# Transposing the second half of x block 0 in the DMA crossbar instead of on TensorE

## The chip, the cores and the metric

The kernel runs on one core of one Trainium2 chip. The metric is device time in microseconds (us) of one execution. The kernel before takes 291.47 us (median of four runs, 291.16 to 291.76).

## The reference

```python
# x: (1, 2048, 576), w1: (576, 4608), b1: (4608), w2: (4608, 576), b2: (576), all bfloat16
def reference(x, w1, b1, w2, b2):
    h = jnp.einsum("bsd,df->bsf", x, w1) + b1
    zero = jnp.zeros_like(h)
    r = jnp.where(h > zero, h, zero)
    h = r * r
    out = jnp.einsum("bsf,fd->bsd", h, w2) + b2
    return out
```

It is two dense layers with a squared ReLU between them. The 2048 rows of x are worked through in four blocks of 512 rows.

## The kernel before

For the first layer TensorE needs x transposed, with the 576 columns of x on partitions. Blocks 1 to 3 come transposed by the DMA crossbar, long before they are needed. Block 0 is needed at once. Its four row tiles of 128 rows come by plain loads, TensorE transposes them (five transposes of 128x128 for each row tile), and VectorE and ScalarE copy the results from PSUM into the tile `xT0`.

```python
    load_x(nc.sync, 0)              # row tile 0 of x, on SyncE's queue
    load_x(nc.scalar, 1)            # row tile 1, on ScalarE's queue
    load_w1n(nc.sync, 0)            # w1n: first 512 columns of w1, one load for each 128 rows
    load_x(nc.scalar, 2)
    load_w1n(nc.sync, 1)
    load_x(nc.sync, 3)
    for k in range(2, NK):          # NK is 4
        load_w1n(nc.sync, k)
# ... cut: b1, b2 loads on GpSimd's queue, constants ...
                def part(h, k):     # half h (256 rows) of block 0, contraction rows k*128 ...
                    hc = slice(h * HS, (h + 1) * HS)
                    for g in range(G):
                        keep(nc.tensor.matmul(banks[g][:, hc], lhsT=w1n[:, k, g * P:(g + 1) * P],
                                              rhs=xT[:, O + k, hc], ...))   # 128x256
                for j in range(2):
                    for k in range(NK):
                        x_transpose(j, k)
                for j in range(2):
                    x_transpose(j, NK)
                x_copies(0)
                part(0, 0)
                for k in range(NK + 1):
                    x_transpose(2, k)
                part(0, 1)
                part(0, 2)
                for k in range(NK + 1):
                    x_transpose(3, k)
                x_copies(1)
                dup_windows(0)
                part(0, 3)
                part(1, 0)
                make_b1T()
                for k in range(1, NK):
                    part(1, k)
# ... then four matmuls over the last 64 rows of w1 (weights w1n8, 64x512), called half-row
#     matmuls below; then a_rows: the rest of layer 1 with the weights w1_h (w_h in the profile)
# ... cut: the loads of w1_h, w1n8, later x blocks and w2, all on SyncE's queue ...
```

A load is *issued* by an engine's queue, which keeps that engine's sequencer busy for some tenths of a microsecond, and it *lands* some microseconds later, when its semaphore has been counted up. SyncE and ScalarE together use eight such semaphores in turn, so the ninth load waits at its issue for the first to land.

## Time and profile before

| | before |
|---|---|
| time, median | 291.47 us |
| span in the profile | 289.8 us |
| TensorE busy | 285.1 us (98%) |
| TensorE transposes of x | 20 |
| first half-row matmul starts | 9.77 us |
| first w_h matmul starts | 10.21 us |

First, lines of the profile's page of the kernel before: the span, the busy time of each engine, the share of each engine in the chain of work that ended last, one group of matmuls (`w1n` parts, with busy time, mean ns of one, and idle time before them), and one group of DMA issues (KB each, median us from issue to landing).

```profile
span 289.8 us, 4679 instructions
...
PE 285.1 (98%) x2017; PEld 133.7 (46%) x2032; DVE 79.5 (27%) x176; ACT 95.2 (33%) x152; POOL 2.8 (1%) x11
...
PE 98%; issue 0%; DVE 0%
...
L228 PE MATMUL pn<-xTw,w1n 128*128 128x256 bf16 x32 | 4.8, 304 | 0.0
...
w1n<-in_w_dram SPq DMA_DIRECT2D x4, 128.0 KB, 3.7
```

The chain is TensorE alone, so only TensorE work removed, or TensorE idle made, moves the time. The 32 half-width matmuls had no idle time before them (0.0).

The timeline of TensorE at the start. The columns are start, us covered, engine, line, operation, output and inputs, shapes, number. A bracket at the end would name idle time and what ended it; there is none.

```profile
3.49 1.25 PE L150 MATMUL tb<-ident,x_sb 128*128 128x128 bf16 x10
4.59 1.01 PE L228 MATMUL pn<-xTw,w1n 128*128 128x256 bf16 x4
5.40 0.74 PE L150 MATMUL tb<-ident,x_sb 128*128 128x128 bf16 x5
5.93 1.39 PE L228 MATMUL pn<-xTw,w1n 128*128 128x256 bf16 x8
7.16 0.44 PE L150 MATMUL tb<-ident,x_sb 128*128 128x128 bf16 x5
7.44 1.04 PE L228 MATMUL pn<-xTw,w1n 128*128 128x256 bf16 x8
...
8.37 1.47 PE L228 MATMUL pn<-xTw,w1n 128*128 128x256 bf16 x12
9.77 0.39 PE L204 MATMUL pn<-xTw,w1n 64*128 64x512 bf16 x1
...
10.21 0.38 PE L189 MATMUL ph<-xTw,w_h 64*128 64x512 bf16 x1
```

From the first part at 4.59 to the half-row matmuls at 9.77 it is 5.18 us. The ten transposes of row tiles 2 and 3 (the two lines x5) take 0.81 us of it in the chain of waits; the 32 matmuls take the other 4.37 us.

Last, windows of one microsecond each. The columns are the busy share of TensorE, its weight loads, VectorE, ScalarE and GpSimd (with numbers of instructions), then the granted TensorE clock, the DMA share and the GB/s. The DMA share adds up the times that packets took, so with packets of two queues in flight on one engine it can pass 1. The clock column needs care at the start: it prints 1.00 wherever the trace has no clock record, and the first record of this trace starts at 6.65 us. Until then TensorE ran at half rate here, as the durations show: up to 6.57 us each 128x256 matmul starts 213 ns after the one before it, from 6.83 us on 109 ns; the transposes follow each other after 107 ns at first and after 56 ns in the last five. So 15 of the 20 transposes and 8 of the 32 matmuls ran at half rate, although the first window prints 1.00.

```profile
4.00:5.00 1.00, 1.00 (x10) 0.86 (x9) 0.51 (x3) 0.65 (x2) 0.00 (x0) 1.00 0.85 231
6.00:7.00 1.00, 1.00 (x9) 0.77 (x7) 0.00 (x0) 0.00 (x0) 0.18 (x1) 1.00 1.17 272
9.00:10.00 1.00, 1.00 (x11) 0.62 (x10) 0.84 (x2) 0.00 (x0) 0.00 (x0) 1.00 0.73 178
```

### The profile page before, as it was taken

How to read it: one execution, taken by the hardware profiler on the slowest of the kernel's cores; microseconds unless marked ns; L12 is line 12 of the kernel's file. 1: busy time of each engine (PE TensorE's matmuls, PEld its weight loads, DVE VectorE, ACT ScalarE, POOL GpSimd, SP SyncE). 2: the span in 40 equal slices, each digit the busy share in tenths (PEclk: the TensorE clock that was granted, in tenths of full speed). 3: DMA queues.
4: the chain of work that ended last, by engine and by line, in shares of the span. 5: the costliest groups of instructions: out<-in, count | busy, mean ns of one | idle time of the engine just before them, and what ended most of it. 6: DMA issues, size and time to landing. Idle time of an engine off the chain costs nothing.

```text
span 289.8 us, 4679 instructions
## 1 busy us (share of the span) xinstructions
PE 285.1 (98%) x2017; PEld 133.7 (46%) x2032; DVE 79.5 (27%) x176; ACT 95.2 (33%) x152; POOL 2.8 (1%) x11
## 2 busy tenths in 40 slices
PE   8999999999999999999999999999999999999996
PEld 5544444444444444444444444444445444444454
DVE  1644554444502100000025444444440000000001
ACT  2666666666500000000027666666670000000000
POOL 3000000000000000000000000000000000000000
PEclk9999999999999999999999999999999999999999
DMA  7999999400001000000000000000000200000000
GB/s 198 213 235 185 315 388 234 83 0 2 0 19 33 5 20 18 18 18 20 18 18 2 1 2 0 2 0 2 0 2 0 38 18 18 18 20 18 20 18 20
DMA packets 30581, 16.26 MB, mean 56 GB/s; under 512 B 14676, under 2 KB 30560, under 8 KB 30560
## 3 DMA queue, kind: packets, MB, share of 16 engines
q1 hardware_dynamic: 30176, 15.65, 21.7%
q8 instruction: 16, 0.26, 0.4%
q10 hardware_dynamic: 288, 0.30, 0.4%
q14 instruction: 5, 0.04, 0.0%
q0 software_dynamic: 96, 0.01, 0.0%
HBM read 11.36 MB, written 2.36 MB: 47 GB/s over the span
## 4 chain that ended last, share of the span: by engine, by line
PE 98%; issue 0%; DVE 0%
PE po L293 43%; PE ph L189 42%; PE pt L272 5%; PE pn L210 4%; PE pn L228 1%; PE wps L63 1%; PE tb L150 1%; PE ph L191 1%; PE pn L204 1%; DVE o_sb L295 0%; PE b1T_ps L167 0%; PE pn L206 0%
## 5 line engine op out<-in xcount | busy, mean ns | idle before, releaser
L191 PE MATMUL ph<-xTw,w_h 64*128 64x512 bf16 x576 | 124.6, 376 | 0.0
L189 PE MATMUL ph<-xTw,w_h 64*128 64x512 bf16 x576 | 124.6, 376 | 0.0
L293 PE MATMUL po<-w_sb,hT 128*128 128x512 bf16 (+2 forms) x600 | 123.8, 366 | 0.8 <-issue 0.3
L177 ACT ACTIVATE r<-ph,b1T 128x512 bf16<-128x512 f32 x128 | 81.0, 684 | 41.7 <-PE ph L191 41.7
L293 PEld LDWEIGHTS <-hT 128*128 128x128 bf16 x612 | 58.3, 98 | 66.7 <-issue 0.8
L189 PEld LDWEIGHTS <-w_h 64*128 64x128 bf16 x576 | 54.1, 94 | 68.3
L178 DVE TENSOR_TENSOR hT<-r 128x512 bf16<-128x512 bf16 x144 | 61.1, 425 | 75.9 <-ACT r L177 75.4
L191 PEld LDWEIGHTS <-w_h 64*128 64x128 bf16 x576 | 54.1, 94 | 0.0
L295 DVE TENSOR_TENSOR o_sb<-po,b_bc 128x512 bf16<-128x512 f32 (+2 forms) x17 | 11.2, 660 | 125.0 <-PE po L293 125.0
L177 ACT ACTIVATE r<-pn,b1T 128x512 bf16<-128x512 f32 x16 | 10.3, 687 | 68.7 <-PE pn L206 67.4
L272 PE MATMUL pt<-hT,w_sb 128*64 128x512 bf16 x144 | 15.9, 380 | 0.0
L272 PEld LDWEIGHTS <-w_sb 128*64 128x64 bf16 x144 | 8.0, 110 | 7.8 <-issue 0.8
L210 PE MATMUL pn<-xTw,w1n 128*128 128x512 bf16 x45 | 10.4, 379 | 0.4 <-issue 0.3
L210 PEld LDWEIGHTS <-w1n 128*128 128x128 bf16 x48 | 4.5, 98 | 6.0 <-issue 0.8
L275 ACT ACTIVATE oT<-pt,b2T 128x512 bf16<-128x512 f32 x2 | 1.4, 687 | 14.5 <-PE pt L272 14.5
L228 PE MATMUL pn<-xTw,w1n 128*128 128x256 bf16 x32 | 4.8, 304 | 0.0
L228 PEld LDWEIGHTS <-w1n 128*128 128x128 bf16 x32 | 3.4, 110 | 0.6
L63 PE MATMUL wps<-const-bfloat16-1.0 128*128 128x512 bf16 (+1 forms) x7 | 2.8, 581 | 0.8 <-PEq L346 0.8
L157 DVE COPY xTw<-tb 128x256 bf16<-128x256 bf16 x4 | 1.1, 292 | 6.6 <-PE tb L150 6.6
L120 DVE COPY xTw<-xTw 64x2048 bf16<-64x2048 bf16 x4 | 2.8, 690 | 0.2
L121 DVE COPY xTw<-xTw 64x2048 bf16<-64x2048 bf16 x4 | 2.7, 687 | 0.1
L159 ACT COPY xTw<-tb 128x256 bf16<-128x256 bf16 x4 | 1.3, 375 | 3.7 <-PE tb L150 3.7
(23 smaller groups left out, 16.9 us busy)
## 6 DMA issues: line engine op xcount, KB each, us to landing
w_sb<-in_w_dram SPq DMA_DIRECT2D x6, 864.0 KB, 9.6
w_h<-in_w_dram SPq DMA_DIRECT2D x14, 288.0 KB, 6.8
out_dram<-o_sb SPq DMA_DIRECT2D x15, 128.0 KB, 1.7
w_h<-in_w_dram SPq DMA_DIRECT2D x4, 144.0 KB, 3.6
w1n<-in_w_dram SPq DMA_DIRECT2D x4, 128.0 KB, 3.7
x_sb<-in_x_dram ACTq DMA_DIRECT2D x2, 144.0 KB, 2.8
x_sb<-in_x_dram SPq DMA_DIRECT2D x2, 144.0 KB, 3.3
out_dram<-ot SPq DMA_DIRECT2D x4, 64.0 KB, 1.8
```

What stands on the lines that cost most here:

```text
L63: keep(nc.tensor.matmul(wps[:, 0:n], lhsT=ones[:, 0:P], rhs=ones[:, 0:n], start=True, stop=True))
L150: keep(nc.tensor.transpose(bank[:, slot, qc], xs[:, j, c0:c0 + P], ident[:]))
L177: keep(nc.scalar.activation(out=r[:], in_=bank[:], func=ACT.Relu, bias=b1T[:, ft:ft + 1], scale=1.0))
L178: keep(nc.vector.tensor_tensor(out=hTs[sb][:, ft, :], in0=r[:], in1=r[:], op=ALU.mult))
L189: keep(nc.tensor.matmul(bx[:], lhsT=w1_h[0:H, LO_C[i], jc], rhs=xT[0:H, LO_W[i], :], start=(i == 0), stop=(i == NC - 1)))
L191: keep(nc.tensor.matmul(by[:], lhsT=w1_h[H:P, UP_C[i], jc], rhs=xT[H:P, UP_W[i], :], start=(i == 0), stop=(i == NC - 1)))
L204: keep(nc.tensor.matmul(banks[2 * i][:], lhsT=w1n8[0:H, i, :], rhs=xT[0:H, SPC, :], start=start, stop=stop, skip_group_check=order == "k_o ...
L210: keep(nc.tensor.matmul(banks[g][:], lhsT=w1n[:, k, g * P:(g + 1) * P], rhs=xT[:, O + k, :], start=start, stop=stop))
L228: keep(nc.tensor.matmul(banks[g][:, hc], lhsT=w1n[:, k, g * P:(g + 1) * P], rhs=xT[:, O + k, hc], start=(h == 0 and k == 0), stop=False, s ...
L272: keep(nc.tensor.matmul(pt[h * DT:(h + 1) * DT, :], lhsT=w2_sb[:, ft, DM:D], rhs=hTs[sb + h][:, ft, :], start=(i == 0), stop=(i == NFT - 1)))
L293: keep(nc.tensor.matmul(po[:, 0:d1 - d0], lhsT=hT[:, ft, jj * P:(jj + 1) * P], rhs=w2_sb[:, ft, d0:d1], start=(i == 0), stop=(i == NFT - 1)))
L295: keep(nc.vector.tensor_tensor(out=o_sb[:, d0:d1], in0=po[:, 0:d1 - d0], in1=b2_bc[:, d0:d1], op=ALU.add))
```

## The change

The intent: TensorE is the bound, and ten of its transposes (0.81 us) are work that the DMA crossbar can do. Rows 256 to 511 of block 0 now come by two transposing loads on ScalarE's queue (256 KB and 64 KB), straight into `xT0`. The two plain loads of these rows go, and so do the copies from PSUM. The GpSimd loads of b1 and b2 move to other queues.

```diff
+    HS = SB // 2
+    alloc_xT(0)
+    xT0 = xT_blk[0]
     load_x(nc.sync, 0)
     load_x(nc.scalar, 1)
-    load_w1n(nc.sync, 0)
-    load_x(nc.scalar, 2)
-    load_w1n(nc.sync, 1)
-    load_x(nc.sync, 3)
-    for k in range(2, NK):
+    keep(nc.scalar.dma_start_transpose(out=xT0[:, O:O + NK, HS:SB], in_=x2[HS:SB, 0:P * NK]))
+    keep(nc.scalar.dma_start_transpose(out=xT0[:, E3:E3 + 1, HS:SB], in_=x2[HS:SB, D - P:D]))
+    for k in range(NK):
         load_w1n(nc.sync, k)
@@ (cut)
-    nc.gpsimd.dma_start(out=b1_rows[0:NFT, :], in_=b1.rearrange("(ft p) -> ft p", p=P))
-    (the two b2 loads on nc.gpsimd: moved behind the w1 loads on nc.sync)
+    keep(nc.scalar.dma_start(out=b1_rows[0:NFT, :], in_=b1.rearrange("(ft p) -> ft p", p=P)))
@@ (cut: PSUM banks of the transposes regrouped; all copies now on VectorE)
-                (transposes of row tiles 2 and 3 between the parts, x_copies(1))
+                for k in (0, 1, 3, 2, NK):
+                    for j in range(2):
+                        x_transpose(j, k)
+                x_copies()
                 dup_windows(0)
-                part(0, 3)
+                for k in (0, 1, 3, 2):
+                    part(0, k)
                 part(1, 0)
                 make_b1T()
```

More of the change, by code (lines that the diff above doesn't have):

```diff
@@ L57 @@
     ps_o = ctx.enter_context(tc.tile_pool(name="ps_o", bufs=4, space=PSUM))
-    wps = ps_o.tile([P, 512], FP32, name="wps", tag="po")
+    wps = ps_h.tile([P, 512], FP32, name="wps", tag="ph")
     ones = nc.const_aps.tensor(1.0, [P, 512], BF16)
@@ L63 @@
         keep(nc.tensor.matmul(wps[:, 0:n], lhsT=ones[:, 0:P], rhs=ones[:, 0:n], start=True, stop=True))
-    xs = const.tile([P, RT, D], BF16, name="x_sb")
+    xs = const.tile([P, RT // 2, D], BF16, name="x_sb")
     w1n = wpool.tile([P, NK, GW], BF16, name="w1n")
@@ L83, in load_w1, with alloc_xT @@
                       in_=w1_v[:, :, GW + h * FH + j0 * P:GW + h * FH + j1 * P]))
+    HS = SB // 2
+    xT_blk = {}
+    def alloc_xT(sb):
+        xT_blk[sb] = xtpool.tile([P, NC, SB], BF16, name="xTw", tag="xTw")
+    E3, O, SPC, E = 0, 1, 5, 6
+    alloc_xT(0)
+    xT0 = xT_blk[0]
     load_x(nc.sync, 0)
     load_x(nc.scalar, 1)
-    load_w1n(nc.sync, 0)
-    load_x(nc.scalar, 2)
-    load_w1n(nc.sync, 1)
-    load_x(nc.sync, 3)
-    for k in range(2, NK):
+    keep(nc.scalar.dma_start_transpose(out=xT0[:, O:O + NK, HS:SB], in_=x2[HS:SB, 0:P * NK]))
+    keep(nc.scalar.dma_start_transpose(out=xT0[:, E3:E3 + 1, HS:SB], in_=x2[HS:SB, D - P:D]))
+    for k in range(NK):
         load_w1n(nc.sync, k)
@@ L97 @@
     nc.gpsimd.memset(b1_rows[:], 0.0)
-    nc.gpsimd.dma_start(out=b1_rows[0:NFT, :], in_=b1.rearrange("(ft p) -> ft p", p=P))
-    b2_col = const.tile([P, 1], BF16, name="b2_col")
-    for h in range(2):
-        nc.gpsimd.dma_start(out=b2_col[h * DT:(h + 1) * DT, :], in_=b2[DM:D].rearrange("(d o) -> d o", o=1))
-    b2T = const.tile([P, 1], FP32, name="b2T")
-    nc.gpsimd.tensor_copy(out=b2T[:], in_=b2_col[:])
+    keep(nc.scalar.dma_start(out=b1_rows[0:NFT, :], in_=b1.rearrange("(ft p) -> ft p", p=P)))
     warm = const.tile([P, 1], FP32, name="warm")
     keep(nc.scalar.activation(out=warm[:], in_=nc.const_aps.tensor(0.0, [P, 1], FP32), func=ACT.Relu))
-    E3, O, SPC, E = 0, 1, 5, 6
     LO_W = [O, O + 1, O + 2, O + 3, E, E + 1, E + 2, E3, SPC]
@@ L111 @@
     UP_C = [1, 3, 5, 7, 8, 2, 4, 6, 0]
-    xT_blk = {}
-    def alloc_xT(sb):
-        xT_blk[sb] = xtpool.tile([P, NC, SB], BF16, name="xTw", tag="xTw")
     def dup_windows(sb):
@@ L137, with x_copies @@
     b2_bc = const.tile([P, D], BF16, name="b2_bc")
-    alloc_xT(0)
-    xT0 = xT_blk[0]
-    HS = SB // 2
-    tb_po = [ps_o.tile([P, 2, HS], BF16, name="tb", tag="po") for _ in range(2)]
-    tb_ph = [ps_h.tile([P, 2, HS], BF16, name="tb", tag="ph") for _ in range(4)]
-    half_banks = [tb_ph, None]
+    tb = [ps_h.tile([P, 2, HS], BF16, name="tb", tag="ph") for _ in range(NK)]
     def x_transpose(j, k):
-        h, q = divmod(j, 2)
-        qc = slice(q * P, (q + 1) * P)
-        bank, slot, c0 = (half_banks[h][k], 0, k * P) if k < NK else (half_banks[h][2], 1, D - P)
+        qc = slice(j * P, (j + 1) * P)
+        bank, slot, c0 = (tb[k], 0, k * P) if k < NK else (tb[2], 1, D - P)
         keep(nc.tensor.transpose(bank[:, slot, qc], xs[:, j, c0:c0 + P], ident[:]))
-    def x_copies(h):
-        hc = slice(h * HS, (h + 1) * HS)
-        for k in range(NK):
-            src = half_banks[h][k][:, 0, :]
-            if k % 2 == 0:
-                keep(nc.vector.tensor_copy(out=xT0[:, O + k, hc], in_=src))
-            else:
-                keep(nc.scalar.copy(out=xT0[:, O + k, hc], in_=src))
-        keep(nc.vector.tensor_copy(out=xT0[:, E3, hc], in_=half_banks[h][2][:, 1, :]))
+    def x_copies():
+        for k in (0, 1, 3, 2):
+            keep(nc.vector.tensor_copy(out=xT0[:, O + k, 0:HS], in_=tb[k][:, 0, :]))
+        keep(nc.vector.tensor_copy(out=xT0[:, E3, 0:HS], in_=tb[2][:, 1, :]))
     b1T = const.tile([P, NFT], FP32, name="b1T")
     def make_b1T():
-        b1T_ps = ps_o.tile([P, P], BF16, name="b1T_ps", tag="po")
+        b1T_ps = ps_h.tile([P, P], BF16, name="b1T_ps", tag="ph")
         keep(nc.tensor.transpose(b1T_ps[:], b1_rows[:], ident[:]))
@@ L199, in a_full @@
         for g in range(G):
-            pool, tag = (ps_o, "po") if g < 2 else (ps_h, "ph")
+            pool, tag = (ps_o, "po") if g < 2 or order == "k_outer" else (ps_h, "ph")
             banks.append(pool.tile([P, SB], FP32, name="pn", tag=tag))
@@ L221, in a_full @@
             if order == "k_outer":
-                tb_new = [ps_h.tile([P, 2, HS], BF16, name="tb", tag="ph") for _ in range(2)]
-                half_banks[1] = tb_new + tb_po
                 def part(h, k):
@@ L230, in part @@
                                               skip_group_check=True))
-                for j in range(2):
-                    for k in range(NK):
+                for k in (0, 1, 3, 2, NK):
+                    for j in range(2):
                         x_transpose(j, k)
-                for j in range(2):
-                    x_transpose(j, NK)
-                x_copies(0)
-                part(0, 0)
-                for k in range(NK + 1):
-                    x_transpose(2, k)
-                part(0, 1)
-                part(0, 2)
-                for k in range(NK + 1):
-                    x_transpose(3, k)
-                x_copies(1)
+                x_copies()
                 dup_windows(0)
-                part(0, 3)
+                for k in (0, 1, 3, 2):
+                    part(0, k)
                 part(1, 0)
@@ L307 @@
         load_w1(nc.sync, 1, j0, j1)
+    b2_col = const.tile([P, 1], BF16, name="b2_col")
+    for h in range(2):
+        keep(nc.sync.dma_start(out=b2_col[h * DT:(h + 1) * DT, :], in_=b2[DM:D].rearrange("(d o) -> d o", o=1)))
+    b2T = const.tile([P, 1], FP32, name="b2T")
+    nc.gpsimd.tensor_copy(out=b2T[:], in_=b2_col[:])
     keep(nc.sync.dma_start(out=b2_bc[:], in_=b2.partition_broadcast(P)))
```

## The prediction

> **What bounds the kernel now.** TensorE. The page's busy table gives PE 285.1 us of a span of 289.8 (98%), granted clock full in every slice, and the chain of waits is 98% PE from start to end. So only PE work removed, or PE idle made, can move the time; the diff touches the first 10 to 15 us alone.
>
> **That start, from the timeline and the chain.** Warm-up matmuls 0.77-3.6; first x rows land about 3.4; 20 transposes of x interleaved with 32 half-width matmuls (128x256); the four half-row matmuls at 9.77; the first w_h matmul at 10.2. In the chain the transposes take 1.14 + 0.53 + 0.28 us, the 32 matmuls 0.86 + 1.19 + 0.87 + 1.31. No PE gaps.
>
> **What the change removes.** Ten transposes, 0.8 us of PE in the chain (0.53 + 0.28). Nine copies on ScalarE and VectorE, two x loads, the GpSimd loads: all hidden.
>
> **What it adds.** Two crossbar transposes on ScalarE's queue (256 + 64 KB). Durations for such issues are in the trace: 512x512 takes 2.4 us to issue and lands 5.0 us after its start in a quiet queue, 512x128 takes 1.25 and lands after 3.0 (SP queue). Half the rows: my estimate from these is 1.2-1.6 us and 0.6-1.0 us of issue, from 1.14 us on. The Trainium skill ("DMA: Bandwidth & Descriptors", Issuing engines are not separate DMA queues) says that both queues share the same 16 engines; the trace agrees: in 2-4 us the two queues take 56% and 43% of DMA that is 99% busy. So I expect the large transpose to land at 5-6 us, the small one at 5.5-6.5.
>
> **New waits.** (a) Part(1,0) needs the large transpose; PE gets there about 7, so little or no stall. (b) The copies of windows need both; 1.38 us on VectorE, done near 8. (c) The subtle one: the records of DMA issues show eight completion semaphores used in turn by SP and ScalarE together; from the ninth load on each issue waits for the load eight before it. Now the second half of the first w_h load (issued 4.34 before) waits for the large transpose and the first w1n8 load (5.01) for the small one. I expect these and the following w_h loads about 1 us later. w1n8's last half landed at 8.2 (5.70 + 2.5); now about 9.2. The third chunk's upper half landed at 13.1, needed near 14.2; now about 14, needed near 13.6.
>
> **On the critical path.** PE alone could reach the half-row matmuls at about 9.0 instead of 9.77 (0.7-0.8 us gained). Late w1n8 gives back about 0.2-0.4, the w_h chunk 0 to 0.5. Net about -0.3 us of 291.75; the three runs spread over 0.6 us.
>
> **Predicted: 291.4 us, 8 in 10 between 290.5 and 292.6.** Faster by over 2%: 0.01; within 2%: 0.97; slower by over 2%: 0.02.
>
> **What would show it right.** Ten transposes (not 20) on PE; first w_h matmul between 9.4 and 10.0 us; a PE gap below 0.6 us before the half-row matmuls whose releaser is the w1n8 load; SP's issue of the second w_h load starting at 5-6 us just after the large transpose lands; later stages unchanged (each output group 10.74 us). A gap before part(1,0) would show the transposes slower than I think.
>
> **What would make it wrong.** The transposes landing at 8 us or later (contention, slow issue on ScalarE): then the w1 loads queue behind them and PE loses 2-3 us, giving about 294. Or the loads landing early enough that no wait arises: then 291.0.

## The result and the profile after

| | before | after |
|---|---|---|
| time, median of four runs | 291.47 us | 294.82 us |
| range | 291.16 to 291.76 | 293.91 to 295.17 |
| span in the profile | 289.8 us | 293.0 us |
| first w_h matmul starts | 10.21 us | 13.23 us |

The ratio of the times is 1.0112, with a 95% interval from 1.0094 to 1.0131. Ratios here are the mean time of one kernel's runs over that of the other's of the same rounds, so they are not quite the ratio of the medians that are quoted. Executions over 1.5% slower than the fastest of the same kernel are left out of the means. The change costs 1.1%: the same at the threshold of 2%, but clearly slower. The measured time lies outside the predicted range of 290.5 to 292.6.

The page of the kernel after, the lines that answer to those of before:

```profile
span 293.0 us, 4667 instructions
...
PE 286.6 (98%) x2022; PEld 133.0 (45%) x2022; DVE 79.3 (27%) x175; ACT 94.1 (32%) x148; POOL 1.0 (0%) x8
...
PE 96%; DMA 3%; DVE 0%; issue 0%
...
L210 PE MATMUL pn<-xTw,w1n 128*128 128x256 bf16 x32 | 5.5, 332 | 2.7 <-DMA w1n<-in_w_dram 2.7
...
w1n<-in_w_dram SPq DMA_DIRECT2D x4, 128.0 KB, 5.5
```

The chain now has 3% DMA. The 32 matmuls waited 2.7 us, and what ended the wait was w1n, a load that the diff hardly touches. Its median landing went from 3.7 to 5.5 us after issue. TensorE's busy time can't be compared as it stands: it rose by 1.5 us, but the trace of the kernel before lacks 15 matmul records (600 of 612 at L293, 45 of 48 at L210), which alone shows as 1.2 us of idle (0.8 and 0.4).

The timeline of the kernel after, the two issues on ScalarE's queue and then TensorE:

```profile
1.18 1.32 ACTq L97 DMA_TRANSPOSE xTw<-in_x_dram  x1
2.53 1.27 ACTq L98 DMA_TRANSPOSE xTw<-in_x_dram  x1
...
3.49 1.26 PE L141 MATMUL tb<-ident,x_sb 128*128 128x128 bf16 x10
4.68 0.61 PE L210 MATMUL pn<-xTw,w1n 128*128 128x256 bf16 x4
7.61 0.71 PE L210 MATMUL pn<-xTw,w1n 128*128 128x256 bf16 x4 [2.32 <-DMA w1n<-in_w_dram]
8.72 2.74 PE L210 MATMUL pn<-xTw,w1n 128*128 128x256 bf16 x12 [0.40 <-DMA w1n<-in_w_dram]
...
11.36 1.50 PE L210 MATMUL pn<-xTw,w1n 128*128 128x256 bf16 x12
12.79 0.39 PE L189 MATMUL pn<-xTw,w1n 64*128 64x512 bf16 x1
...
13.23 0.38 PE L174 MATMUL ph<-xTw,w_h 64*128 64x512 bf16 x1
```

There is a wait of 2.32 us, then one of 0.40 us, and then twelve matmuls take 2.74 us where the last twelve take 1.50. The windows say why:

```profile
4.00:5.00 1.00, 1.00 (x11) 0.83 (x9) 0.91 (x5) 0.33 (x1) 0.00 (x0) 1.00 1.26 96
6.00:7.00 1.00, 0.00 (x0) 0.00 (x0) 0.00 (x0) 0.16 (x1) 0.00 (x0) 1.00 1.22 155
9.00:10.00 1.00, 1.00 (x7) 0.69 (x6) 0.86 (x2) 0.00 (x0) 0.00 (x0) 0.50 0.54 124
```

After the wait the granted clock is 0.50, from 8.0 to 11.4 us. And from 4 to 5 us the DMA engines are busier than before (1.26 against 0.85), but they move 96 GB/s against 231.

The loss adds up. From the first part (4.68) to the half-row matmuls (12.79) it is now 8.11 us. Of this, 2.72 us are the two waits and the other 5.39 us the 32 matmuls, which took 4.37 us before. So the first w_h matmul is later by 2.72 (waits) + 1.02 (matmuls slower in sum) − 0.81 (transposes removed) + 0.09 (later first part) = 3.02 us, which is 13.23 − 10.21. The first matmul of the phase with w2's last columns starts at 79.48 against 76.46 us, again 3.02 us later, and the last matmul ends at 290.10 against 287.08, still 3.02. (The outputs of successive row tiles follow each other after 7.77 us in both kernels; the 10.74 us of the prediction is a piece of 49 matmuls that the chain merged between missing records.) The change costs nothing further after the start, beyond some 0.2 us that lie within the spread of runs.

The clock hides in these sums. An estimate from the spacings above: the half rate up to 6.65 us cost the kernel before about 1.0 us between its first part and its half-row matmuls (0.7 in the matmuls, 0.25 in the transposes), which this profile of the kernel after, at full clock from 4.57 us, did not pay. So the "1.02" is a difference of two losses, and the ten transposes are worth about 0.56 us where the clock is full.

The landings of the first loads, read from the records of DMA issues (issue time, us to landing; the latter is printed to 0.1 us, so the sums are good to 0.05):

| load | before | after |
|---|---|---|
| x row tiles 0 and 1 | 3.43, 3.23 | 3.43, 3.63 |
| w1n 0 | 1.20 + 3.2 = 4.40 | 1.20 + 3.4 = 4.60 |
| w1n 1 | 1.67 + 4.0 = 5.67 | 1.66 + 5.9 = 7.56 |
| w1n 2 | 2.62 + 3.8 = 6.42 | 2.13 + 6.0 = 8.13 |
| w1n 3 | 3.09 + 3.7 = 6.79 | 3.63 + 5.0 = 8.63 |
| transposing, 256 KB | – | 1.18 + 6.7 = 7.88 |
| transposing, 64 KB | – | 2.53 + 5.8 = 8.33 |

w1n 1 was issued at the same time in both kernels, and landed 1.9 us later. The records of the DMA packets, averaged over half-microseconds, show where this comes from. The packets of the w1n loads are of 1024 bytes:

| window | before: 1024-byte packets | after: 1024-byte packets | after: 256-byte packets of the transposing loads |
|---|---|---|---|
| 3.5 to 4.0 | 126, mean 49 ns | 18, mean 148 ns | 319, mean 24 ns |
| 4.0 to 4.5 | 56, mean 48 ns | 20, mean 301 ns | 93, mean 61 ns |
| 4.5 to 5.0 | 60, mean 83 ns | 29, mean 159 ns | 85, mean 45 ns |
| 6.0 to 6.5 | 23, mean 46 ns | 64, mean 125 ns | 96, mean 24 ns |

Plain packets take two to six times as long while transposing packets are in flight on the other queue, and for some of the time the transposing packets stretch too (undisturbed 256-byte packets of them take 18 ns). Groups of long packets of both queues end at nearly the same moments (11, 10 and 6 packets of over 60 ns near 4.06, 4.56 and 5.28 us), as if they waited for one thing; that is suggestive and no more.

### The profile page after: what moved, and what is told of

Read it like the earlier page. It is cut to its first block, busy times and chain, and to the rows that moved or that the text cites. A ratio compares the mean times of both kernels' runs of the same rounds, so it can differ in the third digit from the quotient of the medians.

```text
span 293.0 us, 4667 instructions
## 1 busy us (share of the span) xinstructions
PE 286.6 (98%) x2022; PEld 133.0 (45%) x2022; DVE 79.3 (27%) x175; ACT 94.1 (32%) x148; POOL 1.0 (0%) x8
## 4 chain that ended last, share of the span: by engine, by line
PE 96%; DMA 3%; DVE 0%; issue 0%
PE po L266 43%; PE ph L174 42%; PE pt L245 5%; PE pn L195 4%; DMA w1n<-in_w_dram 2%; PE pn L210 1%; DMA x_sb<-in_x_dram 1%; PE ph L176 1%; PE pn L189 1%; DVE o_sb L268 0%; PE b1T_ps L152 0%; PE pn L191 0%
## 5 line engine op out<-in xcount | busy, mean ns | idle before, releaser
L210 PE MATMUL pn<-xTw,w1n 128*128 128x256 bf16 x32 | 5.5, 332 | 2.7 <-DMA w1n<-in_w_dram 2.7
L210 PEld LDWEIGHTS <-w1n 128*128 128x128 bf16 x32 | 3.5, 118 | 4.4 <-DMA w1n<-in_w_dram 3.4
L191 PE MATMUL pn<-xTw,w1n 64*128 64x512 bf16 x8 | 2.4, 379 | 0.0
```

## The experiments

The theory on trial, X in the records below: transposing packets on one queue that meet plain packets on the other queue slow both, beyond what their bytes would. The rivals: it is only the added bytes on shared engines; it is the turn of the semaphores (Z: the last w1n load is issued at 3.63 instead of 3.09, since it must wait for an x load's semaphore); it is some other edit of the diff; it is only that the transposing packets are small (256 bytes, against 512 of the plain loads that replace them in e1). For this last one no run was made, but c1 below happens to settle it. Experiments named `c` try to rescue the change. Four kernels came back the first time with no chip having run them, and were submitted again, unchanged in what they test, with a `b` in the label (e5b, e6b, e8b, e9b). Fourteen kernels gave a result.

### e1_plain: the same bytes without the transposing

```diff
# against after
-    keep(nc.scalar.dma_start_transpose(out=xT0[:, O:O + NK, HS:SB], in_=x2[HS:SB, 0:P * NK]))
-    keep(nc.scalar.dma_start_transpose(out=xT0[:, E3:E3 + 1, HS:SB], in_=x2[HS:SB, D - P:D]))
+    keep(nc.scalar.dma_start(out=xT0[:, O:O + NK, HS:SB], in_=x2[0:SB, 0:HS].rearrange("(k p) c -> p k c", p=P)))
+    keep(nc.scalar.dma_start(out=xT0[:, E3, HS:SB], in_=x2[HS:HS + P, 0:HS]))
```

The result is wrong (relative error 0.171): the tile gets the same number of bytes, in the same places, from the same queue, but not transposed.

> The two transposing loads of the changed kernel are replaced by plain loads of the same 256 KB and 64 KB into the same places, on the same queue and with the same waits (the result is wrong on purpose). Theory X, interference: transposing packets of one queue and plain packets of the other spoil each other on the shared DMA engines (plain 1024-byte packets took 49 ns before and 100 to 300 ns after). Then w1n lands as early as before, the gaps of TensorE before the 128x256 matmuls (2.3 and 0.4 us after) are below 0.4 us together, and the time is 290.7 to 291.6. Theory Y, mere bytes: any 320 KB put in front of w1n delay it alike; then the gaps stay above 2 us and the time is 294 to 295. Theory Z, the turn of semaphores: the last w1n load is issued at 3.6 us since it waits for an x load; then its issue stays there, a gap of 0.4 to 1 us stays, and the time is near 292.

Measured: 291.4 us, ratio to before 1.0011 (0.9999 to 1.0023). All of the loss is gone. The w1n loads landed 2.9, 3.5, 3.7 and 3.0 us after issue, the clock stayed at 1.0, and the first w_h matmul started at 9.76. The window that was the worst one:

```profile
4.00:5.00 1.00, 1.00 (x10) 0.88 (x9) 0.87 (x5) 0.39 (x2) 0.00 (x0) 1.00 1.11 352
```

The DMA share is 1.11 and the engines move 352 GB/s, against 1.26 and 96 in the kernel after. The 1024-byte packets take 46 to 68 ns. So it is not the bytes. (In this profile the first clock record starts at 6.36 us, so about as many matmuls ran at half rate as in the kernel before.) The semaphores are at most a small part: the last w1n load was again issued late, at 3.53. It landed at 6.53, and a weight load waited 0.61 us for it, another 0.16 us for an earlier one. Matmuls that were still running hid part of this: from the first part (4.49) to the half-row matmuls (9.32) it is 4.83 us, against 4.37 us of matmuls before. So the turn of the semaphores cost at most 0.46 us here, and this is also why e1 starts w_h only 0.45 us earlier than before, and not 0.8 (0.81 for the transposes, plus 0.10 for the earlier first part, less 0.46).

### e2_added: the kernel before with the two transposing loads added

```diff
# against before
     load_x(nc.scalar, 2)
+    spare = const.tile([P, NK + 1, 2 * P], BF16, name="spare")
+    keep(nc.scalar.dma_start_transpose(out=spare[:, 0:NK, :], in_=x2[2 * P:4 * P, 0:P * NK]))
+    keep(nc.scalar.dma_start_transpose(out=spare[:, NK:NK + 1, :], in_=x2[2 * P:4 * P, D - P:D]))
```

Nobody reads `spare`.

> The kernel before, whole, with the two transposing loads added on the ScalarE queue into a tile that nobody reads. X: the x and w1n loads of SP get slow (w1n 5 us or more to landing instead of 3.4 to 3.8), TensorE waits for them 1.5 to 3 us in the first 10 us and the time is 293.5 to 296. Y (only 320 KB more, about 1 us at the 300 GB/s seen in these slices): 292 to 293. If the harm in the changed kernel comes from its new order of work on TensorE and not from the transposing loads: 291.5.

Measured: 296.8 us (295.0 to 297.74), ratio 1.019 (1.0162 to 1.0217). The added loads land 6.9 and 6.5 us after issue, two of the w1n loads 5.7 and 5.9 (these two were also issued later, at 3.53 and 3.90 instead of 2.62 and 3.09), TensorE waits 2.02 us for w1n, and the clock is 0.50 from 8.6 to 12.0 us:

```profile
9.30 1.04 PE L231 MATMUL pn<-xTw,w1n 128*128 128x256 bf16 x4 [2.02 <-DMA w1n<-in_w_dram]
```

Another 0.82 us it waits for a copy on ScalarE, whose sequencer is issuing the two loads until 4.29 us (1.33 and 1.27 us) and reaches its copies late. Added to the kernel before, the two loads are enough to make a loss of this size; their bytes, their issue time and their turns of the semaphores come with them here.

### e3_filler: the kernel after with the clock kept up

```diff
# against after
                     part(0, k)
+                    if k == 0:
+                        fill = ps_h.tile([P, 512], FP32, name="fill", tag="ph")
+                        for _ in range(10):
+                            keep(nc.tensor.matmul(fill[:], lhsT=ones[:, 0:P], rhs=ones[:], start=True, stop=True))
```

The ten matmuls fill the wait, and nobody reads their output.

> The changed kernel with ten matmuls 128x512 of constants after the first four of w1n, that is in the gap from 5.0 to 7.6 us. If the halved clock from 8.0 to 11.3 us (0.50 granted) is a consequence of that gap and costs 1.3 to 1.5 us of its own, the clock stays 1.0, the first w_h matmul starts near 11.8 instead of 13.2 and the time falls to 293.2 to 293.6. If the clock drop costs nothing, because the loads would have held TensorE in any case, the time stays at 294.5 to 295.

Measured: 293.67 us, ratio 1.009 (1.0075 to 1.0104). The clock does not fall: this trace has no clock record at all, but the matmuls keep their full rate (109 ns from one start to the next) through all the parts. In the timeline:

```profile
5.54 2.35 PE L224 MATMUL fill<-const-bfloat16-1.0 128*128 128x512 bf16 x10
...
8.99 1.48 PE L210 MATMUL pn<-xTw,w1n 128*128 128x256 bf16 x12 [0.30 <-DMA w1n<-in_w_dram]
...
12.21 0.38 PE L174 MATMUL ph<-xTw,w_h 64*128 64x512 bf16 x1
```

The twelve matmuls take 1.48 instead of 2.74 us (1.26 less), and the first w_h matmul starts 1.02 us earlier than in the kernel after, although the load that ends the last wait came 0.27 us later here (8.99 against 8.72). So of the loss of 3.3 us the lowered clock is 1.0 to 1.3 us. The runs of the kernel after agree: three with a mean granted clock of 0.993 or 0.994 took 294.78 to 295.17 us, the fourth, with no fall on record, 293.91. The other 2.0 to 2.3 us are what the late loads cost directly, net of the transposes removed.

### e4_order: w1n ahead of the transposing loads in the program

```diff
# against after
     load_x(nc.scalar, 1)
-    keep(nc.scalar.dma_start_transpose(out=xT0[:, O:O + NK, HS:SB], in_=x2[HS:SB, 0:P * NK]))
-    keep(nc.scalar.dma_start_transpose(out=xT0[:, E3:E3 + 1, HS:SB], in_=x2[HS:SB, D - P:D]))
     for k in range(NK):
         load_w1n(nc.sync, k)
+    (the two transposing loads, unchanged, here)
```

> The changed kernel with the four w1n loads ahead of the transposing loads in program order: the queues keep their contents, only the turn of the eight completion semaphores changes. Z: the last w1n load, no more waiting for an x load, is issued at 2.6 us instead of 3.63, lands well before 8.67, and the time falls by 0.4 us or more, to 294.3 or less; if Z were the main cause, to 292. X and Y: the w1n loads still land at 7.5 us and later, the gap of 2.3 us stays, the time is 294.0 to 295.0.

Measured: 294.73 us, ratio 1.0123 (1.0106 to 1.0141), from four runs. It misfired: the order in the program did not change the turn of the semaphores, and the last w1n load was issued at 3.63 as in the kernel after. It is a repeat and tells nothing about Z. It does tell something of the clock. The last three w1n loads landed at 7.4 to 8.5 us, 0.2 earlier than in the profile of the kernel after, and TensorE waited only 1.43 us, yet the first w_h matmul started at 14.12, 0.89 us later:

```profile
7.41 3.83 PE L210 MATMUL pn<-xTw,w1n 128*128 128x256 bf16 x16 [1.43 <-DMA w1n<-in_w_dram]
...
11.14 2.61 PE L210 MATMUL pn<-xTw,w1n 128*128 128x256 bf16 x12
```

The matmuls follow each other after 213 ns up to 13.4 us, and the first clock record starts at 13.45: in this run TensorE never reached its full rate before the wait. So two profiles of one start can differ by about 1 us through the clock alone. For Z, see e1 and e8b: in both the last w1n load is issued late (3.53 and 3.66), at a cost of at most 0.46 us in e1 and with a wait of TensorE of 0.19 us in e8b.

### e8b_rest: all the rest of the diff, without transposing loads

```diff
# against before: warm-up bank, queues of b1 and b2, PSUM banks, copies on VectorE and order of
# the parts as in after; rows 256 to 511 as in before, by plain loads and TensorE
-    nc.gpsimd.dma_start(out=b1_rows[0:NFT, :], ...)
+    keep(nc.scalar.dma_start(out=b1_rows[0:NFT, :], ...))
-                for j in range(2):
-                    for k in range(NK):
+                for k in (0, 1, 3, 2, NK):
+                    for j in range(2):
                         x_transpose(j, k)
# ... cut ...
```

> The changed kernel with all its other edits (no GpSimd loads, copies all on VectorE, other PSUM banks, order of the copies), but with the second half of x loaded plain and transposed by TensorE as before. If the transposing loads are the whole cause, the time is 291.0 to 291.9. If the other edits carry part of the loss, it is 292 or more.

Measured: 291.41 us, ratio 0.9999 (0.9987 to 1.0012). The other edits cost nothing. In the profile the first w_h matmul even starts at 9.69 us, yet the time is that of before; in this profile the full clock began at 4.40 us, 2.25 us earlier than in the profile of the kernel before, which is enough to explain it.

### e6b_bench: the collision measured by itself

```diff
# against before: six cases, each between two output groups of the second layer, twice in a run
+        if n == 0:
+            b_trans(nc.scalar)                 # one transposing load of 256 KB
+        elif n == 1:
+            b_plain(nc.sync, bp)               # two plain loads of 128 KB (w1n's shape)
+        elif n == 2:
+            b_trans(nc.scalar); b_plain(nc.sync, bp)
+        elif n == 3:
+            b_plain(nc.scalar, bq); b_plain(nc.sync, bp)
+        elif n == 4:
+            b_plain(nc.sync, bp); b_trans(nc.sync)
+        elif n == 5:
+            b_trans(nc.sync); b_plain(nc.sync, bp)
```

> The disputed cost by itself. In the kernel before, in the stage of the second product where the DMA engines are nearly idle, loads into unused tiles: (0) the transposing load of 256 KB alone on ScalarE's queue, (1) two plain loads of 128 KB alone on SP's, (2) both at once on the two queues, (3) plain loads on both queues at once, (4) plain and then transposing on SP's queue, (5) transposing and then plain on SP's queue; the whole series twice. X (interference of a transposing and a plain queue): alone, the transposing load lands after 3 to 4 us and plain loads after 2 to 2.5; in (2) the transposing load takes over 4.5 us and the plain loads over 4, with plain packets of 1024 bytes above 100 ns instead of 50; in (3) each plain load lands within 3.2 us; Y (shared bandwidth only): (2) is no slower than (3) by more than 0.7 us. If the harm needs two queues, (4) and (5) show plain packets near 50 ns and landings near the sum of the two alone; if the transposing load harms whatever is near it, (4) and (5) are as slow as (2).

Measured: the transposing load lands 3.3 and 3.2 us after issue alone, 3.9 and 4.3 beside two plain loads. The plain ones land after 2.0 to 2.1 us alone, and up to 3.1 and 3.6 beside it. On one queue it is 3.3 for the transposing load behind plain ones. In the cases with both kinds on two queues, no half microsecond with more than six plain packets averaged over 82 ns. The direction fits X, but the size is far too small: X's forecast was missed. Something of the real start was lacking in the bench.

### e10_bench2: more of the start in the bench

```diff
# against before: as e6b, with both transposing loads (t1: 256 KB, t2: 64 KB) and up to four plain loads
+        elif n == 2:
+            t1(nc.scalar); t2(nc.scalar); w(nc.sync, 4)
+        # ... cut: t1, t2 alone; four plain alone; t1 beside four; plain beside plain; one queue ...
+        elif n == 6:                           # the start as in after: the x loads first
+            xl(nc.sync, 0); xl(nc.scalar, 1)
+            t1(nc.scalar); t2(nc.scalar)
+            w(nc.sync, 4)
```

> The first bench showed only mild harm with 256 KB plain beside 256 KB transposing. Now the loads of the start are repeated in the quiet stage with the start's depth, into unused tiles: (0) both transposing loads alone on ScalarE's queue; (1) four plain loads of 128 KB alone on SP's; (2) both at once; (3) the large transposing load alone with the four; (4) plain loads of 256 and 64 KB on ScalarE's queue with the four; (5) the four and then both transposing loads on SP's queue; (6) the whole set of the start, x loads included; (7) as (2) with two plain loads. If a transposing queue and a deep plain queue hold each other up: in (2) and (6) the last plain load lands after 4.5 us or more and the large transposing load after 5.5 or more, with plain packets above 100 ns; in (4) all lands within 3.7 us, in (5) plain packets stay below 60 ns except where the two kinds meet. If the harm is of the start alone (something else goes on then), (2) and (6) stay mild: transposing below 4.7 us, plain below 3.8.

Measured, as us from issue to landing. A slash parts the first time in the run from the second:

| case | t1 | t2 | plain loads |
|---|---|---|---|
| transposing alone | 3.8 / 3.8 | 2.8 / 2.9 | – |
| four plain alone | – | – | 2.0 to 2.4 |
| both kinds, two queues | 4.3 / 4.6 | 4.2 / 4.2 | 2.1, 3.4, 3.7, 3.8 / 2.2, 3.4, 3.7, 3.7 |
| one queue, plain first | 4.6 / 3.7 | 2.9 / 2.8 | 2.1, 2.5, 3.8, 3.7 / 2.0, 2.1, 2.6, 2.7 |
| four plain beside plain | – | – | at most 3.3 |
| full start, x loads ahead | 6.1 / 8.0 | 5.6 / 7.8 | 2.9, 5.1, 5.2, 5.3 / 3.7, 7.4, 7.4, 7.6 |

Without the x loads the harm is mild. With one plain load on each queue ahead of the rest, the landings of the kernel after appear (6.7 and 5.8; 3.4, 5.9, 6.0, 5.0), in the middle of a run. So the collision needs a backlog: transposing and plain packets that both stand waiting. One thing does not fit: the first time on one queue, the last two plain loads are as late (3.8, 3.7) as on two queues; the second time they are not. (The time of this run, 297.07 us, has no meaning: its last case ran past the end of the kernel.)

### e11_bench3: which part of the full start matters

```diff
# against before: five cases, each twice; x loads first in all but case 2
+        if n == 0:   xl(nc.sync, 0); xl(nc.scalar, 1); t1(nc.scalar); t2(nc.scalar); w(nc.sync, 4)
+        elif n == 1: xl(nc.sync, 0); xl(nc.scalar, 1); plain(nc.scalar);             w(nc.sync, 4)
+        elif n == 2: t1(nc.scalar); t2(nc.scalar); xl(nc.sync, 0); xl(nc.sync, 1);   w(nc.sync, 4)
+        elif n == 3: xl(nc.sync, 0); xl(nc.scalar, 1); t1(nc.scalar);                w(nc.sync, 4)
+        elif n == 4: xl(nc.sync, 0); xl(nc.scalar, 1); w(nc.sync, 4); t1(nc.sync); t2(nc.sync)
```

> In the second bench the full set of the start (x loads ahead on both queues) was slow as in the changed kernel: the large transposing load landed 6.1 and 8.0 us after its issue, the later plain loads 5.1 to 5.3 and 7.4; without the x loads ahead only 4.3 to 4.6 and 3.4 to 3.8. Here, in the same quiet stage, twice each: (0) the full set again; (1) the same set with plain loads of the same bytes in place of the transposing ones; (2) the transposing loads first on ScalarE's queue, both x loads on SP's; (3) the full set without the small transposing load; (4) both transposing loads last on SP's queue. If transposing packets that meet a backlog of plain packets on the other queue hold everything up: (0) 6 us or more again for the large one; (1) all plain loads within 3.8 us; (2) the large one within 4.8 us and w1n within 4.2; (4) w1n within 3.7. If bytes and depth alone do it, (1) is as slow as (0). (3) tells what the small transposing load adds: near (0) if it adds nothing, w1n below 4.2 us if it is the culprit.

Measured, from the DMA issues of three windows of this one run. The columns are tiles, queue, kind, number, KB each, median us to landing. Case 0, the full start:

```profile
bench_p<-in_w_dram SPq DMA_DIRECT2D x4, 128.0 KB, 5.9
...
bench_t<-in_x_dram ACTq DMA_TRANSPOSE x2, 6.5
```

Case 1, the same with plain loads of the same bytes in place of the transposing ones:

```profile
bench_p<-in_w_dram SPq DMA_DIRECT2D x4, 128.0 KB, 3.9
...
bench_t<-in_x_dram ACTq DMA_DIRECT2D x1, 256.0 KB, 4.4
```

Case 4, the transposing loads last on the queue of the plain ones:

```profile
bench_p<-in_w_dram SPq DMA_DIRECT2D x4, 128.0 KB, 3.4
...
bench_t<-in_x_dram SPq DMA_TRANSPOSE x2, 3.4
```

The second time round gave about the same (5.5 to 5.9 for the last three plain loads of case 0, 3.4 to 3.5 for those of case 1, 3.3 to 3.4 for those of case 4). Without the small transposing load (case 3) it is as bad as with it: 6.4 for the large one, 5.4 to 5.9 for the last three plain loads. With the transposing loads first on ScalarE's queue and the x loads on SyncE's (case 2) it is in between: 4.0 to 4.9 for the transposing loads, 3.0 to 4.6 for w1n. Two forecasts were slightly missed: up to 4.1 in case 1 (3.8 was the limit) and 4.6 in case 2 (4.2). So the harm is that of the large transposing load in a backlog on the other queue, and one queue, in order, avoids most of it.

### e5b_sp: both transposing loads on SyncE's queue, behind w1n

```diff
# against after
-    (the two transposing loads on nc.scalar)
     for k in range(NK):
         load_w1n(nc.sync, k)
+    keep(nc.sync.dma_start_transpose(out=xT0[:, O:O + NK, HS:SB], in_=x2[HS:SB, 0:P * NK]))
+    keep(nc.sync.dma_start_transpose(out=xT0[:, E3:E3 + 1, HS:SB], in_=x2[HS:SB, D - P:D]))
```

> The changed kernel with both transposing loads on SP's queue behind the w1n loads, so that one queue alone holds them. If two queues in flight together are the cause: w1n lands by 6 us, no wait for w1n above 0.5 us; the large transposing load, issued at about 3.1, lands at 6.5 to 7.5, and since the w_h and w1n8 loads are issued 2.5 us later than in the kernel before, TensorE waits 0.5 to 1.5 us before the half-row matmuls: 291.3 to 292.8. If a transposing load harms its neighbours on any queue: it lands after 8 and the time is 293.5 or more.

Measured: 293.17 us, ratio 1.0059 (1.0045 to 1.0073), half of the loss gone; my range of 291.3 to 292.8 was just exceeded. w1n lands after 2.9, 3.5, 3.4 and 3.3 us and nothing in the parts waits for it. The transposing loads land after 4.0 and 3.0 us, at 7.08 and 7.46. Their 256-byte packets take 19 to 21 ns. But plain packets slow down here too for a while: 80 ns on average from 3.5 to 4.0 us and 121 ns from 4.0 to 4.5 (against 49 and 48 in the kernel before, 67 and 47 in e1), although no transposing packet runs before 4.98 us. In that time SyncE's sequencer is issuing the large transposing load (3.08 to 4.41); e9b, with the same order, shows it more weakly (76 and 70 ns). So packets in flight together may not be the whole of X; what the issue itself does was not tested. The wait has moved:

```profile
10.00 0.39 PE L189 MATMUL pn<-xTw,w1n 64*128 64x512 bf16 x1 [0.67 <-DMA w1n<-in_w_dram]
10.69 0.39 PE L191 MATMUL pn<-xTw,w1n 64*128 64x512 bf16 x1 [0.30 <-DMA w1n<-in_w_dram]
```

These are the half-row matmuls, and what they wait for are the two w1n8 loads (named w1n in the profile). SyncE's queue issues them at 7.18 and 7.87 instead of 5.01 and 5.70, since the two transposing loads occupy its sequencer for 2.6 us (1.33 and 1.23).

### e9b_sp8: as e5b, with w1n8 ahead of the first w_h loads

```diff
# against e5b
     (the two transposing loads on nc.sync)
+    load_w1n8(nc.sync, 0)
+    load_w1n8(nc.sync, 1)
@@ (removed from their place behind the first w_h loads)
```

> The same as the run before with the two small w1n8 loads ahead of the first w_h loads. If two queues are the cause, the half-row matmuls start at 9.0 to 9.5 us, then up to 1 us of wait for the first w_h loads: 291.0 to 292.0. Else 293 or more.

Measured: 293.4 us, ratio 1.0068 (1.0055 to 1.0081). A miss: the half-row matmuls no longer wait, but the first w_h chunk lands at 11.1 us, and the weight loads of the w_h matmuls wait 2.2 and 0.9 us in sum.

### c1_split: the first w_h chunk and w1n8 early on ScalarE's queue, transposing loads behind w1n on SyncE's

```diff
# against after
     load_x(nc.scalar, 1)
+    load_w1(nc.scalar, 0, 0, 1)
+    load_w1(nc.scalar, 1, 0, 1)
+    load_w1n8(nc.scalar, 0)
+    load_w1n8(nc.scalar, 1)
     for k in range(NK):
         load_w1n(nc.sync, k)
+    (the two transposing loads on nc.sync; the four loads above removed from their old places)
```

> A version meant to beat both: the changed kernel with the transposing loads on SP's queue behind w1n, and the first w_h and the w1n8 loads early on ScalarE's queue, so that their issue no longer waits behind 2.6 us of transposing issues, and nearly all plain packets are through when the transposing packets come. If the harm is two kinds of packets in flight on two queues, and the rest of the loss of the one-queue version was late issue: no wait of TensorE above 0.4 us, half-row matmuls at 9.0 to 9.4 us, 290.6 to 291.2, that is 0.3 to 0.8 us below the kernel before. If the plain loads on ScalarE's queue still meet the transposing ones: the large one lands after 8 and the time is 291.5 to 293.

Measured: 293.18 us, ratio 1.0063 (1.0049 to 1.0076). A miss. The bytes put ahead delay what is needed first: the last w1n load lands at 7.2 us, the transposing loads at 8.8 and 9.3. This run also settles the rival of the small packets. From 3.0 to 5.3 us, before any transposing packet, ScalarE's queue carries plain w_h packets of 256 bytes beside w1n on SyncE's, 100 to 320 in each half microsecond: they take 18 ns each and the 1024-byte packets 46 to 64 ns on average. Small packets on the other queue do not make the harm; transposing ones do.

### c2_first: the transposing loads first on ScalarE's queue, all x and w1n loads on SyncE's

```diff
# against after
-    load_x(nc.sync, 0)
-    load_x(nc.scalar, 1)
     (the two transposing loads on nc.scalar)
-    for k in range(NK):
+    load_x(nc.sync, 0)
+    load_x(nc.sync, 1)
+    for k in (0, 1, 3, 2):
         load_w1n(nc.sync, k)
+    (w1n8 here; parts in the order (0,k), (1,k) for each k; transposes by row tile)
```

> A version meant to beat both: the transposing loads first on ScalarE's queue, before any backlog, all x and w1n loads on SP's queue, w1n8 ahead of w_h, and the 128x256 matmuls of the two halves in turn. If the transposing loads are harmless when they come before the backlog: the large one lands by 5.5 us, w1n by 5.5 to 7, half-row matmuls at 9.0 to 9.6 us, 290.7 to 291.3. If they delay the x loads or w1n even so, TensorE waits another 1 us or more and the time is 292 or more.

Measured: 293.32 us, ratio 1.0067 (1.0051 to 1.0083), from six runs. A miss. The large transposing load is early, at about 5.9 us, but the second x row tile lands at about 5.8, 4.6 us after its issue, and TensorE waits 1.7 to 1.9 us for it and 1.3 us for w_h.

### c3_pool: as e5b, with w1n8 on GpSimd's queue

```diff
# against e5b
     make_identity(nc, ident[:])
+    load_w1n8(nc.gpsimd, 0)
+    load_w1n8(nc.gpsimd, 1)
@@ (removed from nc.sync)
```

> The one-queue version (both transposing loads on SP's queue behind w1n), with the two small w1n8 loads on GpSimd's queue, where they don't wait behind the transposing issues. If the loss that the one-queue version still had (1.8 us) is late issue on SP alone: w1n8 lands by 7 us, no wait before the half-row matmuls, which start at 9.0 to 9.5 us instead of 10.0 and 10.7; the w_h loads are issued 1.35 us earlier than there, but still 0.8 us later than in the kernel before, so 0 to 0.7 us of wait for the third w_h chunk: 291.0 to 292.0. If the loss has another cause (the transposing loads still slow w1n or w_h): 292.5 or more.

Measured: 292.36 us, ratio 1.0024 (1.0011 to 1.0038), the best version with transposing loads, and still slower than before.

```profile
9.35 0.39 PE L191 MATMUL pn<-xTw,w1n 64*128 64x512 bf16 x1
...
14.71 0.39 PE L178 MATMUL ph<-xTw,w_h 64*128 64x512 bf16 x1 [0.66 <-DMA w_h<-in_w_dram]
```

The half-row matmuls start 0.42 us earlier than in the kernel before (9.77). That this is the gain that the change was made for is not shown: in this profile the full clock began at 4.87 us, 1.8 us earlier than in that of the kernel before. At any rate it is lost at 14.71 us, where the third w_h chunk is not there: it was issued at 9.25 and landed 5.4 us later.

### c4_gate: as c3, with half of the second w_h chunk on ScalarE's queue

```diff
# against c3
+    gate = const.tile([P, 1], BF16, name="gate")          # ScalarE waits here for the small transposing load
+    keep(nc.scalar.copy(out=gate[:], in_=xT0[:, E3, HS:HS + 1]))
-        load_w1(nc.sync, 1, j0, j1)
+        load_w1(nc.scalar if j0 == 1 else nc.sync, 1, j0, j1)
```

> As the run before, with one half of the second w_h chunk (144 KB) issued on ScalarE's queue, where it waits for the small transposing load to land (a copy of one column before it), so that it meets no transposing packets and SP's later w_h loads are issued 0.65 us earlier. If the about 1 us that TensorE waited at 14.7 us for the third chunk was the whole rest of the loss, that wait falls below 0.3 us, the half-row matmuls stay at 9.3 to 9.5 us, and the time is 290.9 to 291.6, level with the kernel before or up to 0.2% below it. If not, 292 or more.

Measured: 292.93 us (292.62 to 296.1, that one run with a mean granted clock of 0.994), ratio 1.0071 (1.0034 to 1.0109). One run of the kernel before in these rounds took 1078.72 us, which tells nothing.

```profile
14.91 0.39 PE L178 MATMUL ph<-xTw,w_h 64*128 64x512 bf16 x1 [0.84 <-DMA w_h<-in_w_dram]
```

A miss that tells something: the third chunk's load was issued 0.7 us earlier (8.56) and landed no earlier (6.3 us after issue). That points to the DMA engines, and not the issue, as what the third w_h chunk waits for in these versions. No version that I ran beats the kernel before.

## Why the prediction was wrong

- **Right: the bound and the place.** TensorE is the bound, and the whole difference arises before the first w_h matmul (3.02 us there, the same 3.02 us at 79.48 us). Ten of twenty transposes are gone, and they took 0.81 us of the kernel before, as predicted. The prediction read the clock as full in every slice of the page; that row counts time without a record as full, and five of the ten ran at half rate (0.53 us against 0.28).
- **Wrong: the step that failed.** It is "So I expect the large transpose to land at 5-6 us, the small one at 5.5-6.5", together with the silent assumption that w1n would land as before. They landed at 7.88 and 8.33, and w1n 1, 2 and 3 landed 1.7 to 1.9 us later than before. The estimate started from transposing loads of later blocks, in a quiet queue (5.0 and 3.0 us; in the same trace such loads of 512x512 also landed after 7.2 and 10.7 us, issued at 18.73 and 39.37 us), and from the Trainium skill ("DMA: Bandwidth & Descriptors", Issuing engines are not separate DMA queues), which says that loads from all queues run on the same 16 engines and interleave. The trace agrees that the engines are shared. It does not agree that sharing is all: the same bytes on the same queue by plain loads (e1) leave w1n at 2.9 to 3.7 us, the transposing ones make it 5.9 and 6.0, with plain packets of 301 ns instead of 48.
- **The skill elsewhere.** "Advanced Engine Details and Errata", X-Bar Transpose (TRN2), says "TRN2 transpose DMAs are as fast as regular DMAs". Alone, nothing here speaks against it: 256 KB landed after 3.2 to 3.8 us, and a plain load of 256 KB beside four others took 3.3 (e10; none was timed alone). In a backlog of plain packets from the other queue it is not so: 6.1 to 8.0 us, where a plain load of the same bytes in the same place takes 3.5 to 4.4 (e11, case 1).
- **Wrong: "little or no stall" at the parts.** I looked for a wait at part(1,0), which reads the transposed rows. The wait arose earlier, 2.32 + 0.40 us at parts that read only rows of the old way, through weights that the diff hardly touches.
- **Not foreseen: the clock.** TensorE idled for 2.32 us, and then the granted clock was 0.50 for 3.4 us. That cost 1.0 to 1.3 us (e3 took it away). The Trainium skill ("TensorE: Matmul & The Clock Gate", Part 1) has the clock fall after an idle window of about 3.4 us. Here the clock records show full clock for 3.42 us (4.57 to 7.99) and then the fall, with 2.32 us of idle in that stretch; in e2 full clock for 3.42 us (5.21 to 8.63) with 2.16 us of idle in it (0.82 and 1.34). A wait of 1.68 us in c2 was followed by no fall.
- **Partly right: the semaphore turn.** The second w_h load was issued at 7.88, the very moment the large transposing load landed. But the half-row matmuls started at 12.79 with no wait. I also missed that b1's load, now on ScalarE's queue, takes a turn, so that the last w1n load is issued at 3.63; in the kernel after this can have cost no more than the second wait, 0.40 us, and in e1 it cost at most 0.46 us.
- **Wrong in size: the small load's issue.** Predicted 0.6 to 1.0 us, measured 1.27. It bound nothing here, but it did in e5b.
- **The alternative that I named** ("landing at 8 us or later ... about 294") came true in its size, for another reason: not loads queued behind the transposing ones, but loads beside them.
- **The gain.** In the profile the first w_h matmul starts 0.45 us earlier in e1 and 0.52 us earlier in e8b, and in e1 TensorE ends about 0.4 us earlier. The times show none of it (ratios 1.0011 and 0.9999). In e8b, which removes no transposes, the earlier clock is enough to explain it. In e1 and e5b the clock was close to that of the kernel before (first records at 6.36 and 6.58 us, against 6.65): without its wait e5b would have reached the half-row matmuls at about 9.3 us, as e1 did (9.32), so some 0.45 us of the predicted 0.7 to 0.8 were there to be had in these profiles. Why the times of e1 show none of it stays open.

What is shown: the transposing of the large load, in a backlog across two queues, makes the late landings, and with them the loss (e1, e2, e10, e11; c1 for the packet size). What stays open is why the DMA engines do this. The packets' common end times suggest that they wait for one thing, and the slow plain packets in e5b before any transposing packet suggest that the issue has a part in it, but no run here isolates either.

## What to carry to other kernels

Before a transposing load goes to a second queue, look at what the plain loads on the other queue will be doing in the same microseconds: it is their landing, not its own, that may bind. If it must be early, put it behind the urgent loads on their own queue and count its issue time (1.2 to 1.3 us here) against everything issued after it. Cost a TensorE wait at more than its length: a wait of 2.3 us cost another 1.0 us or more through the clock (one of 1.68 us did not). And before you compare two profiles of the start of a kernel, compare the time from one matmul to the next in both: here the full clock began anywhere from 4.1 to 6.7 us, once only at 13.45, and that alone moves the first microseconds by up to 1 us.

## What the Trainium skill lacked or had wrong

- "DMA: Bandwidth & Descriptors", Rules for kernel authors: "A transpose next to ordinary DMAs needs nothing". For correctness all runs here agree (all results but the one made wrong were correct). For time it needs care: plain 1024-byte packets went from about 48 to up to 301 ns on average, and plain loads of 128 KB landed 5.9 us after issue where they had landed after 4.0 us before, and after 3.5 us beside plain loads of the same bytes (e1).
- "DMA: Bandwidth & Descriptors", Queues, rings and completion order: it has each engine go round the queues with work packet by packet. Such alternation alone does not explain 96 GB/s at a DMA share of 1.26 against 352 GB/s at 1.11 with plain packets: one undisturbed packet of each kind, 1280 bytes in 46 + 18 ns on each of 16 engines, would be about 320 GB/s (an estimate from the packet times of these traces). No page has the slowdown.
- "Advanced Engine Details and Errata", X-Bar Transpose (TRN2): "as fast as regular DMAs" lacks its condition. 256 KB transposed took 3.2 to 3.8 us alone, 3.3 to 4.6 in order behind plain loads on one queue (e5b, e6b, e10, e11), and 6.1 to 8.0 us against a backlog on the other queue.
- "DMA: Bandwidth & Descriptors", Issuing engines are not separate DMA queues: it calls the issue time usually small beside the DMA itself. A transposing load of 256 KB held the issuing sequencer for 1.32 us and one of 64 KB for 1.27, against 0.42 for a plain load of 128 KB; in e5b that made w1n8 late, and in e2 it made ScalarE's copies late by 0.82 us.
- "TensorE: Matmul & The Clock Gate", Part 1: the fall to half clock came at the end of a stretch of 3.42 us in which TensorE was idle for 2.32 us (2.16 in e2), and not only after an idle window of about 3.4 us as the page's table has it; the half clock then lasted 3.41 us in both.
